# Blocks 3 and 4 of a state-space and Mish kernel: VectorE copies all partial sums of the projection, five rotations stand behind it, and GpSimd issues block 4's x after the stores of weight sums

## The chip, the cores and the metric

The kernel runs on one core of a Trainium2 chip. The metric is device time in microseconds (us) of one execution; the median of several executions counts. In the text PE is the matrix engine (TensorE), DVE is VectorE, ACT is ScalarE, POOL is GpSimd and SP is SyncE, which here issues DMA transfers only. Each of the five works through its own list of instructions strictly in the order in which the program gave them; they meet by semaphores.

## The reference

The input x has 2048 tokens of 1024 channels. With a layer norm over the channels, xn = (x - mean) / sqrt(var + eps), the result is the sum of three parts:

```
Bu   = xn @ B_bar^T                         # complex: two real projections, 1024 -> 1024 each
h[t] = Lam_bar * h[t-1] + Bu[t]             # a recurrence along the tokens, one complex state per channel
y    = 2 * real(h @ C^T) + xn * Dskip
m    = act @ w2,  act = hh * tanh(softplus(hh)),  hh = xn @ w1 + b1      # 1024 -> 3584 -> 1024
out  = x + y + m
```

## The kernel before, in words

**Blocks.** The 2048 tokens are worked in four blocks of 512; the code counts them as `blk` 0 to 3, the text calls them blocks 1 to 4. The change touches blocks 3 and 4 (`blk in SPLIT`, L183) and, for one group of transfers, block 2 (`blk == FAST`, which is 1).

**Stages of block 3 or 4 on PE.** (1) `first_tile` (L812): the first 12 of 28 tiles of xn @ w1, eight products of 512 columns each (L821). ACT writes tiles 0 to 6 with their bias into `hb` (L831), DVE tiles 7 to 11 (L834). (2) `project_fast` (L1124): the complex projection and the other 16 tiles of w1, both by a scheme that makes seven half-size products where eight would be plain (L901 for the projection, L972 for w1). (3) `dense` (L1214): act @ w2, 28 tiles f one after the other into all eight PSUM banks (L1211 with `act`). (4) `proj` (L1229): h @ C^T, eight channel groups j, into the same banks (L1211 with `hT`). (5) `finish` (L1274): DVE adds x, ACT issues the store.

**The order inside project_fast** is a string of tokens written out by hand (L185 to L188), and each engine's list follows it. `a` to `d` with a digit is one product of the projection, eight matmuls of 256 columns; each letter stands for two channel groups j. `w` to `z` with a digit is the same for four tiles of w1, with weights from `ring`. The digit says which of the seven products it is: 2, 1 and 5 open a bank, 6, 7, 4 go on in bank X behind product 1, and 3 goes on in bank Z behind 5. Before PE may go on in a bank, its partial sum must have been read out. That is done right behind the product, in `evacuate` (L905) or `w_evacuate` (L979): products 1, 5 and 6 are copied to a slot of `snaps`, products 1, 3 and 7 end with an addition on DVE (L926 or L1009), product 4 is copied out. For letters a and b the copies are DVE's (L916, L943), for c and d they are ACT's (L918, L945). For w to z most copies are ACT's (L992), a few DVE's (L995).

The other tokens: `r` n is `rotate_in` (L865), four DVE operations that turn channel group n by a table (L867 twice, L870, L872); `t1` is the tanh of the second chain (below); `g` n is a whole chain on ACT; `m` n multiplies a group of tiles on DVE (L859); `u` n lets PE do the first six tiles of `dense` for bank n.

```
HEAD = "a2 a1 b2 b1 a5 b5 a6 b6 a3 b3 a7 b7 c2 d2 a4 b4 c5 c1 r0 d5 d1 r1 c6 c3 d6"
PARTS = HEAD + (" t1 d3 c7 w1 d7 w5 w2 c4 d4 w6 r2 x1 x5 x2 w7 w3 r3 m0 x6 w4 y1 y5 y2 x7 x3 r4 m1 y6 x4"
                " z1 z5 g2 z2 y7 y3 z6 y4 u0 z7 u2 z3 u1 z4 u7 g3 r5 r6 r7")
```

**Chains** (`chain`, L844) make the activation on ACT for a group of tiles of `act`: Exp, Ln, Tanh, each over the whole group (L853). The groups are tiles 0 to 6, 7 to 11, 12 to 19 and 20 to 27. Chain 0 is called behind tile 6 of stage 1, chain 1 without its Tanh behind tile 11, chains 2 and 3 as g2 and g3.

**Behind project_fast** the main loop calls `recur(blk, j)` for j = 0 to 7 (L1173): two scans (L1176) and four operations that turn the state back (L1181, L1184, L1186), all on DVE. Behind recur 0 stands `chain_mul(2)`, behind recur 3 `chain_mul(3)` (L859): the products that `dense` reads as tiles f = 12 to 19 and f = 20 to 27.

**Block 2 prepares the weights** of the seven-product form. `w_load` brings raw parts of w1 into `hb` and `act`, `w_scale` (L1100) scales them on ACT, `w_sums` (L1108) makes sums and differences on DVE (L1120), and each result is stored to DRAM as `wsd` by a DMA that POOL issues (`w_store`, L1095, L1097). Parts for w1's third set lie in tiles 0 to 7 of `act`, so chain 0 of block 3 may write there only when those stores have landed. At the end of block 2 the calls come in this order: `w_scale(3)`, then `tail`'s rest, which ends with four loads of block 4's x issued by POOL (`load_x`, L360, called at L1311) into the tiles from which block 2's result is being stored, then `w_sums(2)` and `w_sums(3)` with four stores each, then block 3's `sums_x` (L1392): four subtractions on POOL into `TT` (L1395), which the projection reads.

Of the kernel before, what the change touches and what calls it, by code (L numbers as in the profile page):

```python
# [6 lines left out]
AF = mybir.ActivationFunctionType  # L7
# [156 lines left out]
def build_kernel(nc, A_x, A_Lambda_re, A_Lambda_im, A_B_re, A_B_im, A_C_re, A_C_im,  # L164
# [6 lines left out]
    NB = S // TB  # L171
    NQ = TB // P
# [8 lines left out]
    FAST = 1  # L181
# [2 lines left out]
    GROUPS = ((0, 7), (7, NPL), (NPL, NPL + 8), (NPL + 8, NF))  # L184
    HEAD = "a2 a1 b2 b1 a5 b5 a6 b6 a3 b3 a7 b7 c2 d2 a4 b4 c5 c1 r0 d5 d1 r1 c6 c3 d6"  # L185
    WHOLE = HEAD + " t3 d3 c7 d7 u7 c4 r2 u5 d4 u6 u4 r3 r4 r5 r6 r7 m2 m3"
    PARTS = HEAD + (" t1 d3 c7 w1 d7 w5 w2 c4 d4 w6 r2 x1 x5 x2 w7 w3 r3 m0 x6 w4 y1 y5 y2 x7 x3 r4 m1 y6 x4"
                    " z1 z5 g2 z2 y7 y3 z6 y4 u0 z7 u2 z3 u1 z4 u7 g3 r5 r6 r7")  # L188
    NWQ = (NF - NPL) // 4
    W_SEQ = [("wxyz".index(o[0]), int(o[1])) for o in PARTS.split() if o[0] in "wxyz"]  # L190
    W_BANKS = ((3, 5, 7), (1, 5, 6), (4, 5, 7), (3, 5, 6))
# [5 lines left out]
    PO = Queue(nc, "po")  # L197
# [162 lines left out]
    def load_x(queue, blk, q):  # L360
        r0 = blk * TB + q * P
        i = blk % 2
        queue.dma(lambda e: e.dma_start(xx[:, i, q, :], A_x[0, r0:r0 + P, :]),  # L363
                  s_xx[i][q] if blk else s_x0[q], writes=[b_xx[i][q]])
# [197 lines left out]
    def b1(f):  # L562
        return par[:, 3 * NJ + f:3 * NJ + f + 1]
# [43 lines left out]
    def w1_tile(base, f, k):  # L607

        s = (base + 2 * (f // 4) + k // (NK // 2)) % NRING
        wt = ring[:, s, :].rearrange("p (k f) -> p k f", k=NK // 2)  # L610
        return s, wt[:, k % (NK // 2), (f % 4) * P:(f % 4 + 1) * P]
# [185 lines left out]
    def mish_tanh(g):  # L797
        a = act[:, g * GF:(g + 1) * GF, :]
        aop(lambda e: e.activation(a, a, AF.Tanh), reads=[b_act[g]], writes=[b_act[g]])
# [8 lines left out]
    def item_done():  # L808
        n_item[0] += 1
        ring_load()  # L810

    def first_tile(blk, f):  # L812
        bank, hs = f % 8, f % (2 * GF)
        if blk in SPLIT:
            bank = (0, 1, 2, 3, 5, 1, 4, 0, 6, 2, 3, 7)[f]
        raw = blk == 0 and f < NR
        if raw:
            first_rest(f)
        for k in range(0 if raw else NK):
            s, w = w1_tile(n_item[0], f % 4, k)  # L820
            PE.mm(lambda e, k=k, w=w: e.matmul(ps[:, bank, :], lhsT=w, rhs=xnT[:, k, :],  # L821
                                               start=k == 0, stop=k == NK - 1),
                  reads=[b_ring[s]] + b_xnT, writes=[b_ps[bank]], first=k == 0, last=k == NK - 1)
        if f % 4 == 3:
            item_done()
            item_done()
        if f % GF == 0 and f >= 2 * GF:
            mish_mul(f // GF - 2)
        ts = slice(2 * P if raw else 0, 4 * P)
        if blk and f < GF:  # L830
            aop(lambda e: e.activation(hb[:, hs, :], ps[:, bank, :], AF.Identity, bias=b1(f)),  # L831
                reads=[b_ps[bank], b_par], writes=[b_hbf[hs]])
        else:
            vop(lambda e: e.tensor_scalar(hb[:, hs, ts], ps[:, bank, ts], b1(f), None, op0=ALU.add),  # L834
                reads=[b_ps[bank], b_par], writes=[b_hbf[hs]])
        if blk in SPLIT:
            if f == GF - 1:
                chain(0)
            if f == NPL - 1:
                chain(1, (0, 1))  # L840
        elif f % GF == GF - 1:
            mish(f // GF, hold=blk >= FAST and f == NF - 1)

    def chain(g, passes=(0, 1, 2)):  # L844
        lo, hi = GROUPS[g]
        i = lo - NPL if lo >= NPL else lo
        h, b_h = hb[:, i:i + hi - lo, :], b_hbf[i:i + hi - lo]
        a, b_a = act[:, lo:hi, :], b_actf[lo:hi]
        if lo >= NPL:
            h, b_h, a, b_a = a, b_a, h, b_h  # L850
        for n in passes:
            src, b_src, fn, bias = ((h, b_h, AF.Exp, 0.0), (a, b_a, AF.Ln, 1.0), (a, b_a, AF.Tanh, 0.0))[n]
            aop(lambda e, src=src, fn=fn, bias=bias: e.activation(a, src, fn, bias=bias), reads=b_src, writes=b_a)  # L853

    def chain_mul(g):
# [46 lines left out]
                    ps[:, bank, o:o + TH], lhsT=w, rhs=x, start=opens and begin, stop=end, skip_group_check=True),  # L902
                    reads=[b_w] + b_x, writes=[b_ps[bank]], first=begin, last=end, chained=not opens)

    def evacuate(pr, n, keep):  # L905
        X, Y, Z = (4 * ((pr + 1) % 2) + i for i in range(3))
        j0 = 2 * pr

        def bank(b):
            return ps[:, b, :].rearrange("p (j t) -> p j t", j=2)  # L910

        def snap(b):
            i = free_snaps.pop(0)
            dst = snaps[:, 2 * i:2 * i + 2, D - TH:D]
            if pr < 2:
                vop(lambda e: e.tensor_copy(dst, bank(b)), reads=[b_ps[b]], writes=[b_snap[i]])  # L916
            else:
                aop(lambda e: e.copy(dst, bank(b)), reads=[b_ps[b]], writes=[b_snap[i]])  # L918
            return dst, i

        def join(b, kept, ci, th):
            src, i = kept
            b_src = b_snap[i]
            free_snaps.append(i)
            dst = hT16[:, ci, j0:j0 + 2, th * TH:(th + 1) * TH]
            vop(lambda e: e.tensor_tensor(dst, bank(b), src, op=ALU.add),  # L926
                reads=[b_ps[b], b_src], writes=b_hT[ci][j0:j0 + 2])

        if n == 1:
            keep[pr, "a"] = snap(X)  # L930
            join(Y, keep[pr, "a"], 0, 0)
        if n == 5:
            keep[pr, "e"] = snap(Z)
        if n == 6:
            keep[pr, "v"] = snap(X)
        if n == 3:
            join(Z, keep[pr, "v"], 0, 1)
        if n == 7:
            join(X, keep[pr, "e"], 1, 1)
        if n == 4:  # L940
            dst = hT16[:, 1, j0:j0 + 2, 0:TH]
            if pr < 2:
                vop(lambda e: e.tensor_copy(dst, bank(X)), reads=[b_ps[X]], writes=b_hT[1][j0:j0 + 2])  # L943
            else:
                aop(lambda e: e.copy(dst, bank(X)), reads=[b_ps[X]], writes=b_hT[1][j0:j0 + 2])  # L945
# [162 lines left out]
    def w_sums(i):  # L1108
        (rl_, b_rl_), (rh_, b_rh_), (il_, b_il_), (ih_, b_ih_) = (w_unit(w_raw(i, ci, kh))
                                                                  for ci in range(2) for kh in range(2))  # L1110
        (s1, b_s1), (s2, b_s2), (s4, b_s4), (s3, b_s3) = (w_unit(u) for u in w_sum_at(i))
        for n, o, b_o, x, b_x, y, b_y, op in ((5, s1, b_s1, il_, b_il_, ih_, b_ih_, ALU.add),
                                              (6, s2, b_s2, s1, b_s1, rl_, b_rl_, ALU.subtract),
                                              (3, s4, b_s4, rh_, b_rh_, s2, b_s2, ALU.subtract),
                                              (7, s3, b_s3, rl_, b_rl_, il_, b_il_, ALU.subtract)):
            if n == 3:
                y = y.bitcast(f16)
            if n == 6:
                x = x.bitcast(f16)
            vop(lambda e, o=o, x=x, y=y, op=op: e.tensor_tensor(o.bitcast(f16), x, y, op=op),  # L1120
                reads=b_x + b_y, writes=b_o)
            w_store(i, n, o, b_o)

    def project_fast(order, open_unit):  # L1124
        keep = {}
        split = order is PARTS
        w_pos[0] = 0
        for o in order.split():
            kind, n = o[0], int(o[1:])
            if kind == "r":  # L1130
                rotate_in(n)
            elif kind == "u":
                open_unit(n)
            elif kind == "m":
                (chain_mul if split else mish_mul)(n)
            elif kind == "t":
                if split:
                    chain(n, (2,))
                else:
                    mish_tanh(n)  # L1140
            elif kind == "g":
                chain(n)
            elif kind in "wxyz":
                w_product("wxyz".index(kind), n)
                w_evacuate("wxyz".index(kind), n, keep)
            else:
                product("abcd".index(kind), n)
                evacuate("abcd".index(kind), n, keep)

    def project_in():  # L1150
        for j in range(NJ):
# [53 lines left out]
    def tail(blk, base):  # L1205
# [89 lines left out]
        if ends:  # L1295

            for h in range(2):
# [7 lines left out]
                r0 = blk * TB + 3 * P  # L1305
                out_events["end", h] = (SP, AC)[h].dma(lambda e, lo=lo, r0=r0: e.dma_start(
                    out[0, r0:r0 + P, lo:lo + 256], xx[:, i, 3, lo:lo + 256]), DmaSem(nc, "d_end%d" % h), reads=[b_end[h]])
        if blk >= FAST:
            for _ in range(njt):
                item_done()  # L1310
        if blk + 2 < NB:  # L1311
            for q in range(NQ):
                load_x(PO, blk + 2, q)

# [91 lines left out]
    for blk in range(NB):  # L1406
# [37 lines left out]
        if blk in SPLIT:  # L1444
            project_fast(PARTS, open_unit)
        elif blk:
# [75 lines left out]
        if blk == FAST:  # L1522
            w_sums(2)
            w_sums(3)
        if blk == FAST - 1:
            snaps_ready()

# [35 lines left out]
```

## Time and profile before

| | |
|---|---|
| median of 3 runs | 612.12 us (611.13 to 612.88) |
| the profiled execution | 611.5 us, its span 610.3 us |
| PE busy | 598.6 us, 98% |
| DVE busy | 489.5 us, 80% |
| ACT busy | 399.1 us, 65% |
| POOL busy | 124.3 us, 20% |
| the chain that ended last | PE 90%, DMA 3%, ACT 3%, DVE 2%, issue 2% |
| PE's waits over the whole span | for ACT's copies (L918) 5.0 us, once; for DVE 1.0 us and for DMA 0.9 us, both at the start |

A row of a timeline gives the start in us, the time in us, the engine, the line, the operation, the tiles that it writes and reads, how many were merged into the row, and in brackets how long the engine had been idle before it and what ended that. Within a merged row the operations follow on one another. Matmuls overlap: eight of 256 columns take 0.87 us from the start of the first to the start of what follows, though the row says 1.04.

### The profile page before, as it was taken

The page shows a single profiled execution, that of the slowest core. Times are in us where ns is not written, and L with a number is a line of the kernel's source. Part 1 is how long each engine was busy: PE and PEld are TensorE (multiplying, and loading weights), DVE is VectorE, ACT ScalarE, POOL GpSimd, SP SyncE. Part 2 cuts the span into 40 slices and gives each one's busy share as a digit, 9 for nine tenths or more (in the row PEclk, how much of TensorE's full clock was granted, in tenths as well). Part 3 has the DMA queues.
Part 4 walks back from the last instruction along what each step waited for, and adds up shares of the span by engine and source line. Part 5 has one row for each costly group of instructions (what it writes and reads, how often), then busy time and mean ns, then how long its engine had stood idle before and what let it go on. Part 6 is the DMA issues. An engine that isn't in the chain of part 4 may idle for free.

```text
span 610.3 us, 8878 instructions
## 1 busy us (share of the span) xinstructions
PE 598.6 (98%) x3393; PEld 334.9 (55%) x3439; DVE 489.5 (80%) x758; ACT 399.1 (65%) x376; POOL 124.3 (20%) x137
## 2 busy tenths in 40 slices
PE   8999999999999999999999889999999999999998
PEld 7644444444444586444445778644444688844444
DVE  6999999999998969969687468799707567789923
ACT  4589998389879898294572977995302968892000
POOL 2899300221025000610448000000004200000000
PEclk9999999999999999999999989999999999999999
DMA  8999996991795401899899118655666404854421
GB/s 247 253 279 272 244 172 183 293 294 60 216 330 179 170 21 31 261 303 275 230 389 407 53 36 273 212 172 169 173 192 199 163 1 144 286 192 142 166 73 69
DMA packets 103236, 119.36 MB, mean 196 GB/s; under 512 B 52890, under 2 KB 74010, under 8 KB 103194
## 3 DMA queue, kind: packets, MB, share of 16 engines
q1 hardware_dynamic: 93424, 91.05, 52.0%
q0 software_dynamic: 6080, 19.41, 9.5%
q10 hardware_dynamic: 3690, 8.34, 3.7%
q8 instruction: 27, 0.44, 0.3%
q14 instruction: 15, 0.12, 0.1%
HBM read 90.98 MB, written 15.73 MB: 175 GB/s over the span
## 4 chain that ended last, share of the span: by engine, by line
PE 90%; DMA 3%; ACT 3%; DVE 2%; issue 2%; SPq 1%; POOL 0%; ACTq 0%; DVEq 0%
PE ps L1211 49%; PE ps L821 17%; PE ps L901 9%; PE ps L972 8%; PE ps L1155 5%; ACT act L853 2%; DMA wsd<-act 2%; DMA ring<-in_B_w_dram 1%; PE ps L626 1%; DVE act L1120 1%; PE ps L617 0%; ACT L853 0%; DVE act L995 0%; POOL wsd L1097 0%; SPq L363 0%
## 5 line engine op out<-in xcount | busy, mean ns | idle before, releaser
L1211 PE MATMUL ps<-ring,act 128*128 128x512 bf16 x876 | 193.8, 379 | 1.1
L1211 PEld LDWEIGHTS ps<-ring,act 128*128 128x128 bf16 x896 | 87.7, 98 | 103.3
L821 PE MATMUL ps<-xnT,ring 128*128 128x512 bf16 x571 | 125.8, 379 | 0.7
L821 PEld LDWEIGHTS ps<-xnT,ring 128*128 128x128 bf16 x584 | 57.2, 98 | 68.7 <-DMA ring<-in_B_w_dram 0.2
L1211 PE MATMUL ps<-ring,hT 128*128 128x512 bf16 x369 | 81.6, 379 | 0.5
L1211 PEld LDWEIGHTS ps<-ring,hT 128*128 128x128 bf16 x378 | 37.0, 98 | 44.6
L1176 DVE TENSOR_TENSOR_SCAN hT<-cs,qi,hT 128x512 bf16<-128x512 f32 x48 | 58.9, 1267 | 0.0
L834 DVE TENSOR_SCALAR hb<-ps,par 128x512 bf16<-128x512 f32 (+1 forms) x59 | 39.3, 708 | 10.7 <-PE ps L821 10.2
L831 ACT ACTIVATE hb<-ps,par 128x512 bf16<-128x512 f32 x21 | 13.8, 689 | 45.2 <-PE ps L821 45.2
L1181 DVE TENSOR_TENSOR mt<-hT,tab 128x1024 bf16<-128x1024 bf16 x64 | 41.4, 688 | 1.1
L1395 POOL TENSOR_TENSOR TT<-xnT 128x1024 f16<-128x1024 bf16 x6 | 15.1, 2516 | 132.5 <-DVE mt L551 132.5
L1279 DVE TENSOR_TENSOR xx<-ps,xx 128x1024 bf16<-128x1024 f32 (+1 forms) x16 | 18.6, 1187 | 25.5 <-PE ps L1211 25.5
L926 DVE TENSOR_TENSOR hT<-ps,snaps 128x512 f16<-128x512 f32 x36 | 24.2, 688 | 14.2 <-ACT snaps L918 11.1
L972 PE MATMUL ps<-TT,ring 128*128 128x256 f16 x256 | 32.2, 273 | 0.0
L867 DVE TENSOR_TENSOR mt<-hT,tab 128x1024 bf16<-128x1024 f16 x48 | 30.9, 684 | 0.3
L792 ACT ACTIVATE act<-hb 128x3584 bf16<-128x3584 bf16 x8 | 25.5, 3184 | 6.8 <-DVE hb L834 6.8
L853 ACT ACT_TABLE_LOAD x18 | 23.1, 1283 | 10.3 <-DMA wsd<-act 10.0
L992 ACT ACTIVATE snaps<-ps,par,wsm 128x256 f32<-128x256 f32 x44 | 23.7, 560 | 8.9 <-PE ps L972 8.1
L901 PE MATMUL ps<-TT,SS 128*128 128x256 f16 x192 | 24.3, 279 | 5.0 <-ACT snaps L918 5.0
L853 ACT ACTIVATE hb<-hb 128x4096 bf16<-128x4096 bf16 x8 | 28.9, 3617 | 0.1
L1009 DVE SCALAR_TENSOR_TENSOR act<-ps,wsm,snaps 128x512 bf16<-128x512 f32 x24 | 17.8, 749 | 13.4 <-PE ps L972 9.8
L1155 PE MATMUL ps<-xnT,BT 128*128 128x512 bf16 x126 | 27.7, 379 | 0.1
(187 smaller groups left out, 973.2 us busy)
## 6 DMA issues: line engine op xcount, KB each, us to landing
ring<-in_B_w_dram SPq DMA_DIRECT2D x96, 512.0 KB, 4.5
ring<-wsd SPq DMA_DIRECT2D x28, 512.0 KB, 4.7
ring<-ctd SPq DMA_DIRECT2D x24, 512.0 KB, 3.5
wsd<-act POOLq DMA_DIRECT2D x20, 256.0 KB, 7.9
ctd<-act ACTq DMA_DIRECT2D x8, 512.0 KB, 4.3
out_dram<-xx ACTq DMA_DIRECT2D x15, 256.0 KB, 5.9
xx<-in_A_x_dram POOLq DMA_DIRECT2D x12, 256.0 KB, 6.2
act<-in_A_B_re_dram POOLq DMA_DIRECT2D x8, 256.0 KB, 5.1
```

What stands on the lines that cost most here:

```text
L792: aop(lambda e: e.activation(a, hs, AF.Exp), reads=[b_hb[g % 2]], writes=[b_act[g]])
L821: PE.mm(lambda e, k=k, w=w: e.matmul(ps[:, bank, :], lhsT=w, rhs=xnT[:, k, :], start=k == 0, stop=k == NK - 1), reads=[b_ring[s]] + b_xnT, ...
L834: vop(lambda e: e.tensor_scalar(hb[:, hs, ts], ps[:, bank, ts], b1(f), None, op0=ALU.add), reads=[b_ps[bank], b_par], writes=[b_hbf[hs]])
L853: aop(lambda e, src=src, fn=fn, bias=bias: e.activation(a, src, fn, bias=bias), reads=b_src, writes=b_a)
L867: vop(lambda e, s=s: e.tensor_tensor(mt[:, s, :, :], hT16[:, :, j, :], tab[:, s, j, :].unsqueeze(1).to_broadcast([P, 2, TB]), op=ALU.mult) ...
L901: PE.mm(lambda e, w=w, x=x, o=o, begin=begin, end=end: e.matmul(ps[:, bank, o:o + TH], lhsT=w, rhs=x, start=opens and begin, stop=end, ski ...
L926: vop(lambda e: e.tensor_tensor(dst, bank(b), src, op=ALU.add), reads=[b_ps[b], b_src], writes=b_hT[ci][j0:j0 + 2])
L972: PE.mm(lambda e, w=w, x=x, o=o, begin=begin, end=end: e.matmul(ps[:, bank, o:o + TH], lhsT=w, rhs=x, start=opens and begin, stop=end, ski ...
L1155: PE.mm(lambda e, j=j, ci=ci, k=k, bank=bank: e.matmul(ps[:, bank + ci, :], lhsT=BT[:, ci, j, k, :], rhs=xnT[:, k, :], start=k == 0, stop= ...
L1176: vop(lambda e, ci=ci, init=init: e.tensor_tensor_scan(out=hT[:, ci, j, :], data0=cj("r", j).to_broadcast([P, TB]), data1=hT[:, ci, j, :], ...
L1181: vop(lambda e, s=s: e.tensor_tensor(mt[:, s, :, :], hT[:, :, j, :], tab[:, s, j, :].unsqueeze(1).to_broadcast([P, 2, TB]), op=ALU.mult), ...
L1211: PE.mm(lambda e: e.matmul(ps[:, u, :], lhsT=lhsT, rhs=rhs, start=st_, stop=last), reads=reads, writes=[b_ps[u]], first=st_, last=last, te ...
```

## The change

The tokens t1 and r0 to r7 of PARTS move, for blocks 3 and 4 only. Before, r0 and r1 stood among the products of c and d, r2, r3 and r4 among those of w, x and y, and r5, r6, r7 at the end. After, r0, r1 and r2 stand in the three places among w, x and y, and r3 to r7 at the end. The Tanh of chain 1 follows its Exp and Ln at once. In these two blocks DVE makes the copies for c and d as well. Block 2 keeps its order and its engines (`split` is false there). POOL's four loads of block 4's x are issued after the eight stores of `w_sums(2)` and `w_sums(3)`.

```diff
-    PARTS = HEAD + (" t1 d3 c7 w1 d7 w5 w2 c4 d4 w6 r2 x1 x5 x2 w7 w3 r3 m0 x6 w4 y1 y5 y2 x7 x3 r4 m1 y6 x4"
-                    " z1 z5 g2 z2 y7 y3 z6 y4 u0 z7 u2 z3 u1 z4 u7 g3 r5 r6 r7")
+    PARTS = ("a2 a1 b2 b1 a5 b5 a6 b6 a3 b3 a7 b7 c2 d2 a4 b4 c5 c1 d5 d1 c6 c3 d6"
+             " d3 c7 w1 d7 w5 w2 c4 d4 w6 r0 x1 x5 x2 w7 w3 r1 m0 x6 w4 y1 y5 y2 x7 x3 r2 m1 y6 x4"
+             " z1 z5 g2 z2 y7 y3 z6 y4 u0 z7 u2 z3 u1 z4 u7 g3 r3 r4 r5 r6 r7")
...
             if f == NPL - 1:
-                chain(1, (0, 1))
+                chain(1)
...
-    def chain(g, passes=(0, 1, 2)):
+    def chain(g):
...
-        for n in passes:
-            src, b_src, fn, bias = ((h, b_h, AF.Exp, 0.0), (a, b_a, AF.Ln, 1.0), (a, b_a, AF.Tanh, 0.0))[n]
+        for src, b_src, fn, bias in ((h, b_h, AF.Exp, 0.0), (a, b_a, AF.Ln, 1.0), (a, b_a, AF.Tanh, 0.0)):
...
-    def evacuate(pr, n, keep):
+    def evacuate(pr, n, keep, on_v):
...
-            if pr < 2:
+            if on_v:
                 vop(lambda e: e.tensor_copy(dst, bank(b)), reads=[b_ps[b]], writes=[b_snap[i]])
             else:
                 aop(lambda e: e.copy(dst, bank(b)), reads=[b_ps[b]], writes=[b_snap[i]])
...
-            if pr < 2:
+            if on_v:
                 vop(lambda e: e.tensor_copy(dst, bank(X)), reads=[b_ps[X]], writes=b_hT[1][j0:j0 + 2])
...
             elif kind == "t":
-                if split:
-                    chain(n, (2,))
-                else:
-                    mish_tanh(n)
+                mish_tanh(n)
...
                 product("abcd".index(kind), n)
-                evacuate("abcd".index(kind), n, keep)
+                evacuate("abcd".index(kind), n, keep, split or kind in "ab")
...
-        if blk + 2 < NB:
+        if blk + 2 < NB and blk != FAST:
             for q in range(NQ):
                 load_x(PO, blk + 2, q)
...
         if blk == FAST:
             w_sums(2)
             w_sums(3)
+            for q in range(NQ):
+                load_x(PO, blk + 2, q)
```

## The prediction

> **What bounds the kernel now.** I read the page's busy times first, then PE's waits, then the timelines of PE, ACT and DVE around the one long wait. PE is busy for 598.6 of 610.3 us and waits once: 5.0 us for ACT's copies (L918), in block 3's projection. PE's timeline there, then block 4's at the same place:
>
> ```profile
> 331.03 3.66 PE L901 MATMUL ps<-xnT,BT 128*128 128x256 bf16 x32
> ...
> 347.62 1.04 PE L901 MATMUL ps<-xnT,BT 128*128 128x256 bf16 x8
> 353.67 1.89 PE L901 MATMUL ps<-TT,SS 128*128 128x256 f16 x8 [5.01 <-ACT snaps L918]
> 355.35 1.53 PE L901 MATMUL ps<-xnT,SS 128*128 128x256 bf16 x8
> ...
> 359.34 1.04 PE L972 MATMUL ps<-xnT,ring 128*128 128x256 bf16 x8
> ...
> 483.10 3.66 PE L901 MATMUL ps<-xnT,BT 128*128 128x256 bf16 x32
> ...
> 504.94 1.04 PE L972 MATMUL ps<-xnT,ring 128*128 128x256 bf16 x8
> ```
>
> From a2, the first product, to w1, the 26th, block 4 takes 504.94 - 483.10 = 21.84 us (0.873 per product) and block 3 takes 359.34 - 331.03 = 28.31. So the wait costs **6.47 us**, more than its length: c6, the 21st, was due at 331.03 + 20 x 0.873 = 348.49 and began at 353.67, 5.18 late; the other 1.29 come behind it, where c6 and c3 run slower. The clock says why: granted 1.00 in 348 to 352 us, 0.62 in 352 to 356, 0.96 in 356 to 360. ACT is late because its chain 0 began late:
>
> ```profile
> 333.29 1.28 ACT L853 ACT_TABLE_LOAD   x1 [10.01 <-DMA wsd<-act]
> ...
> 350.31 2.34 ACT L853 ACTIVATE act<-act 128x2560 bf16<-128x2560 bf16 x1
> 352.56 2.03 ACT L918 COPY snaps<-ps 128x512 f32<-128x512 f32 x4
> ...
> 358.39 1.28 ACT L853 ACT_TABLE_LOAD   x1
> 359.69 2.34 ACT L853 ACTIVATE act<-act 128x2560 bf16<-128x2560 bf16 x1
> ```
>
> The copies for c and d stand behind two chains (333.29 to 352.56), and these behind stores of weight sums (the chain that ended last: issue 321.75, landing 11.38 us later).
>
> **Edit 1: DVE makes the copies for c and d.** Per block eight operations leave ACT (0.58 each) and go to DVE (0.69 each, row L916), and r0 and r1 leave the same stretch. DVE then has 7 operations of about 0.66 per letter, 4 x 7 x 0.66 = 18.5 us against PE's 28 x 0.873 = 24.4. Followed one by one, with 0.19 us from a product's end to DVE's start (a1: 332.78 to 332.97): c1 ends at 346.74, its copy at 347.62, and c6, which goes on in that bank, is due at 348.49. The worst stretch (d5, d1, c6) leaves d6's and c7's banks free 0.6 and 1.1 us early. So PE's wait goes, and with it the slow clock. What is late next? ACT's first copy for w1, which w6 (32nd product, 358.1 without the wait) needs. With chain 0 at the old 333.29, ACT ends chain 1's Ln at 352.56, its Tanh, now at once, 3.54 us later (358.39 to 361.93 in the old place) at 356.10, and w1's copies at 357.2. That is 0.9 us early even if edit 3 brings nothing. In block 4 ACT is 8 us ahead and nothing waited: no gain. Term: **-6.47 us**. Bounds: 0 if another wait takes the place, -6.5 in full.
>
> **Edit 2: five rotations at the end instead of three.** DVE's list is in order, and at the end of project_fast it starts level with PE: the operation ahead of the rotations waits for the last product, z4. Before:
>
> ```profile
> 390.50 1.12 DVE L995 TENSOR_SCALAR act<-ps,wsm,par 128x256 bf16<-128x256 f32 x2 [1.42 <-PE ps L972]
> 391.54 1.28 DVE L867 TENSOR_TENSOR mt<-hT,tab 128x1024 bf16<-128x1024 f16 x2
> ...
> 393.65 1.29 DVE L867 TENSOR_TENSOR mt<-hT,tab 128x1024 bf16<-128x1024 f16 x2
> ...
> 395.77 1.29 DVE L867 TENSOR_TENSOR mt<-hT,tab 128x1024 bf16<-128x1024 f16 x2
> ...
> 402.26 2.28 DVE L859 TENSOR_TENSOR act<-act,hb 128x4096 bf16<-128x4096 bf16 x1
> ...
> 417.94 2.28 DVE L859 TENSOR_TENSOR act<-act,hb 128x4096 bf16<-128x4096 bf16 x1
> ```
>
> ```profile
> 390.29 44.62 PE L1211 MATMUL ps<-ring,act 128*128 128x512 bf16 x202
> 434.75 2.54 PE L1211 MATMUL ps<-ring,hT 128*128 128x512 bf16 x10
> ```
>
> DVE has no idle time from 390.50 to the second multiplication (L859), so the two added rotations, 2 x 2.115 = 4.23 us (391.54 to 393.65 to 395.77), move everything behind them by 4.23. Who waits? PE's dense stage reads tiles 12 to 19 after the first L859 and 20 to 27 after the second. It runs from 390.29 to 434.75, 206 matmuls in program order (6 for u7, 24 for the four other banks of tiles 0 to 5, then 8 per tile; four records are missing), 0.2158 us each. Tile 12 is matmul 78: 390.29 + 78 x 0.2158 = 407.12. The first L859 ends at 404.54: 2.58 us of room. Tile 20 is matmul 142: 420.93. The second ends at 420.22: **0.71 us of room**. With 4.23 more and 0.05 to release, PE waits 1.7 us at tile 12 (408.82 - 407.12); by tile 20 it is that much later and waits 1.9 more. Together 4.23 - 0.71 + 0.05 to 0.15 = 3.6 us. Block 4 has the same distances (dense from 535.89, L859 ending at 550.14 and 565.82): 3.6 again. Nothing later is hurt: the scans feed `proj`, which needs j = 0 at 434.75 and has it at 402.3, and j = 5 to 7 at 452, when recur 7 has ended at 438.5 (both now some 4 us later). Block 4's transposes of xn move from 435.4 to about 440, wanted at 462.5. Term: 2 x 3.6 = **+7.2 us**, bounds 6.0 to 8.0 (rooms misread by 0.3).
>
> **Edit 3: loads of x behind the stores.** POOL's list at the place:
>
> ```profile
> 313.67 0.54 POOL L1097 DMA_DIRECT2D wsd<-act  x1 [0.82 <-ACT act L1103]
> 314.20 0.54 POOL L363 DMA_DIRECT2D xx<-in_A_x_dram  x1
> ...
> 319.61 0.55 POOL L363 DMA_DIRECT2D xx<-in_A_x_dram  x1 [1.18 <-DVE mt L551]
> 320.14 4.27 POOL L1097 DMA_DIRECT2D wsd<-act  x8
> 324.43 2.14 POOL L1395 TENSOR_TENSOR TT<-xnT 128x1024 f16<-128x1024 bf16 x1
> ```
>
> The loads wait for block 2's output stores, and the eight wsd stores stand behind them although DVE has their data from 312.3 on (L1120). Moved ahead, the stores go at 314.2 to 318.5, the four loads at 318.5 to 320.6, and TT begins near 320.7 instead of 324.4 (it is first read by a5 at 334.5). The store that chain 0 waits for is issued near 315.8 instead of 321.75, and with 8 to 11 us to land chain 0 starts at 324 to 328 instead of 333.3. The x loads land before 330 and are read at 408. But by edit 1 the PE no longer cares when chain 0 starts, so: 0 us, bounds -0.1 and +0.9, the last if SP's ring loads land later in the fuller queue (DMA is near its full share from 304 to 336 us anyway, with POOL's queue never empty).
>
> **Sum.** 611.5 - 6.47 + 7.2 + 0 = 612.2 for the profiled execution. The median of the runs is 0.6 above that execution, so 612.8. The gain is real and given back later, by chance almost to the microsecond. With the terms' bounds and the spread of single runs (611.13 to 612.88) this case covers 611.0 to 614.5.
>
> **Rivals.** (a) *Clock*: the four new waits of 1.7 to 1.9 us close the clock gate as the 5.01 us did. Price up to 4 x 1.29 = 5.2: 618.0, slower. For it: a wait here did lower the clock. Against: the first ring wait of 0.69 us, near 6.9 us, left it at 1.00, and during the long wait it still stood at 1.00 in 348 to 352. The new waits are nearer to 0.69 than to 5.01; I take 0. The point is how much idle time the gate bears. The Trainium skill, "TensorE: Matmul & The Clock Gate", "What's actually happening", has half clock after an idle window of about 3.4 us, which the new waits don't fill; its section on a second failure mode, in which short idles make the clock swing, speaks against this change and would give the 618.0. (b) *The head still waits*, on DVE or on w1's copies: the 6.47 stay, 619.3 in full. Against: the rooms of 0.6 to 1.1 us above. (c) *The rotations cost PE nothing*, since multiplications come earlier than I place them: 612.1 - 6.5 = 605.6. For it: the page's idle PE time would allow it. Against: DVE starts level with z4 and nothing idles behind it. (d) *Edit 3 does not bring chain 0 forward*, the queue being as long as before: same time as the forecast.
>
> **Chances.** Forecast with (d) 0.72, (a) 0.09, (b) 0.08, (c) 0.11. About 0.3%, 1.8 us, can be told from no change. Within the forecast case, 0.60 is no change, 0.10 slower (above 613.9), 0.02 faster. Faster 0.02 + 0.11 = 0.13; slower 0.10 + 0.09 + 0.08 = 0.27; same 0.60. The range, 611.0 to 618.0, leaves out (c) and the full price of (b).
>
> **What would show it.** In the profile after: no wait of PE for L918 or any copy in block 3, a2 to w1 in 21.8 us; four waits of PE for DVE's multiplication (L859) in the dense stages, near 1.7, 1.9, 1.7, 1.9 us; DVE's five rotations back to back; the wait of ACT for wsd down from 10 us to under 5. Wrong would be: dense stages without waits (c), a clock under 1.00 behind the short waits (a), or a new releaser in block 3's head (b).

## The result and the profile after

The changed kernel takes 615.32 us (median of 17 runs, 612.03 to 620.77) against 612.57 of the kernel before (17 runs, 609.26 to 617.77). The ratio is **1.0054, 95% interval 1.0028 to 1.0081**: about 3.3 us slower (1.7 to 5.0). The forecast was 612.8 with "no change" likeliest; the time lies within the stated range of 611.0 to 618.0, but above the 611.0 to 614.5 of the forecast case, and the difference is beyond the 1.8 us that were to count as no change. The profiled execution took 614.75 us, its span is 613.5.

PE's waits of the changed kernel (engine, line, who released it, us in total, times, longest):

```profile
PE ps L1208 <- DVE act L859: 6.6, 4, 1.7
PE ps L822 <- DMA ring<-in_B_w_dram: 2.3, 1, 2.3
PE ps L580 <- DVE filler L412: 1.0, 1, 1.0
...
```

The last row shown and those left out are waits in the first 12 us. The wait for ACT's copies is gone, and four waits for DVE's multiplication have come, as forecast. The second row was not forecast: in block 3's first tiles PE waits for a ring load of w1. The timeline of PE, the three places after one another:

```profile
327.44 6.22 PE L822 MATMUL ps<-xnT,ring 128*128 128x512 bf16 x28 [2.27 <-DMA ring<-in_B_w_dram]
333.50 3.66 PE L901 MATMUL ps<-xnT,BT 128*128 128x256 bf16 x32
...
350.96 1.04 PE L901 MATMUL ps<-TT,SS 128*128 128x256 f16 x8
...
355.33 1.04 PE L972 MATMUL ps<-xnT,ring 128*128 128x256 bf16 x8
...
404.87 13.99 PE L1208 MATMUL ps<-ring,act 128*128 128x512 bf16 x64 [1.58 <-DVE act L859]
420.55 13.99 PE L1208 MATMUL ps<-ring,act 128*128 128x512 bf16 x64 [1.70 <-DVE act L859]
434.38 27.79 PE L1208 MATMUL ps<-ring,hT 128*128 128x512 bf16 x128
```

Read it against the timeline shown before. From a2 to w1 PE now takes 355.33 - 333.50 = 21.83 us, where it took 28.31: 6.48 gained. From w1 to the first matmul on `hT` it takes 434.38 - 355.33 = 79.05, where it took 434.75 - 359.34 = 75.41: 3.64 lost; in block 4 the dense stage loses 3.61 (48.08 us against 44.47). A wait in the brackets is counted from the modelled end of the last matmul, 0.16 us behind its place in the stream, so 1.58 + 1.70 + 2 x 0.16 = 3.60. And a2 starts at 333.50 where it started at 331.03, though tile 0 starts alike (310.33 and 310.31): 2.45 lost to the ring load. The sum is -6.48 + 3.64 + 3.61 + 2.45 = +3.22, and the spans of the two profiled executions differ by 3.2. Nothing is left over.

DVE at the end of block 3's project_fast, the rows that stand for those shown of before:

```profile
386.49 1.12 DVE L995 TENSOR_SCALAR act<-ps,wsm,par 128x256 bf16<-128x256 f32 x2 [1.42 <-PE ps L972]
387.54 1.28 DVE L867 TENSOR_TENSOR mt<-hT,tab 128x1024 bf16<-128x1024 f16 x2
...
389.65 1.29 DVE L867 TENSOR_TENSOR mt<-hT,tab 128x1024 bf16<-128x1024 f16 x2
...
396.02 1.29 DVE L867 TENSOR_TENSOR mt<-hT,tab 128x1024 bf16<-128x1024 f16 x2
...
402.52 2.28 DVE L859 TENSOR_TENSOR act<-act,hb 128x4096 bf16<-128x4096 bf16 x1
...
418.21 2.28 DVE L859 TENSOR_TENSOR act<-act,hb 128x4096 bf16<-128x4096 bf16 x1
```

It still starts level with z4 (a wait of 1.42 for PE), then five rotations follow back to back from 387.54. From 387.54 to the first L859 it is 14.98 us, before 402.26 - 391.54 = 10.72. ACT of the changed kernel:

```profile
322.62 0.69 ACT L832 ACTIVATE hb<-ps,par 128x512 bf16<-128x512 f32 x1 [1.04 <-PE ps L822]
323.59 1.28 ACT L853 ACT_TABLE_LOAD   x1 [0.28 <-DMA wsd<-act]
...
344.26 2.34 ACT L853 ACTIVATE act<-act 128x2560 bf16<-128x2560 bf16 x1
356.41 1.16 ACT L992 ACTIVATE snaps<-ps,par,wsm 128x256 f32<-128x256 f32 x2 [9.81 <-PE ps L972]
```

Chain 0 starts 9.7 us earlier: ACT writes the last of its input (tile 6) until 323.31 and then waits only 0.28 us for the store, where it waited 10.01. Once both chains are done, ACT stands idle for 9.8 us. That is the gain of the third edit, at a place where no one waits.

### The profile page after: what moved, and what is told of

It is laid out like the page before. It is cut to its first block, busy times and chain, and to the rows that moved or that the text cites. A ratio compares the mean times of both kernels' runs of the same rounds, so it can differ in the third digit from the quotient of the medians.

```text
span 613.5 us, 8910 instructions
## 1 busy us (share of the span) xinstructions
PE 600.6 (98%) x3439; PEld 334.2 (54%) x3439; DVE 503.7 (82%) x774; ACT 391.0 (64%) x360; POOL 123.8 (20%) x137
## 4 chain that ended last, share of the span: by engine, by line
PE 84%; DVE 11%; DMA 4%; SPq 1%; issue 0%
PE ps L1208 39%; PE ps L822 18%; PE ps L901 12%; PE ps L972 8%; PE ps L1152 5%; DMA ring<-in_B_w_dram 4%; DVE hT L1173 3%; DVE mt L867 2%; DVE mt L1178 2%; DVE act L859 1%; PE ps L627 1%; DVE hT L870 1%; DVE hT L872 1%; DVE hT L1181 1%; PE ps L618 0%; DVE hT L1183 0%
## 5 line engine op out<-in xcount | busy, mean ns | idle before, releaser
L1208 PE MATMUL ps<-ring,act 128*128 128x512 bf16 x896 | 196.0, 379 | 6.6 <-DVE act L859 6.6
L832 ACT ACTIVATE hb<-ps,par 128x512 bf16<-128x512 f32 x21 | 13.8, 691 | 45.8 <-PE ps L822 45.8
L1208 PE MATMUL ps<-CT,hT 128*128 128x512 bf16 x128 | 27.8, 379 | 0.0
L972 PEld LDWEIGHTS ps<-TT,ring 128*128 128x128 f16 (+1 forms) x256 | 25.0, 98 | 3.8
```

The costliest lines, as they stand in the source:

```text
L972: PE.mm(lambda e, w=w, x=x, o=o, begin=begin, end=end: e.matmul(ps[:, bank, o:o + TH], lhsT=w, rhs=x, start=opens and begin, stop=end, ski ...
L1208: PE.mm(lambda e: e.matmul(ps[:, u, :], lhsT=lhsT, rhs=rhs, start=st_, stop=last), reads=reads, writes=[b_ps[u]], first=st_, last=last, te ...
```

## The experiments

The theory after the result: three terms, copies on DVE -6.5, rotations at the end +7.2, loads behind the stores +2.4. The rivals: the late ring load is jitter; or DVE's lateness comes from the copies and not from the rotations. Eight kernels take the terms apart. All ratios are to the kernel before on the same chip.

**loads_back**: the changed kernel, third edit undone.

```diff
-        if blk + 2 < NB and blk != FAST:
+        if blk + 2 < NB:
...
             w_sums(3)
-            for q in range(NQ):
-                load_x(PO, blk + 2, q)
```

> The changed kernel with one part undone: the loads of block 4's x are issued ahead of the stores of w_sums(2) and w_sums(3) again. Theory (sum of three terms: copies on DVE -6.5, two more rotations at the end +7.2, loads behind the stores +2.4 by a late ring load of w1 in block 3's first tiles): the DMA wait of PE near tile 8 of block 3 goes (0.3 us or less), the four waits for L859 stay at 6.6 us in the view of waits, chain 0 of block 3 begins near 333 us again without PE waiting for it; about 0.7 us above the kernel before, 2.4 below the changed kernel. Rival (the late ring load is jitter of single executions and has nothing to do with the order of POOL's list): as the changed kernel, 2.5 to 3 us above the kernel before, with the DMA wait there again.

Measured: 612.14 us, ratio 1.0007 (0.9989 to 1.0026). PE's waits:

```profile
PE ps L1208 <- DVE act L859: 6.5, 4, 1.7
PE ps L580 <- DVE filler L412: 1.0, 1, 1.0
```

The wait for the ring load is gone and the waits for DVE are there in full. Chain 0 starts at 332.94, late as in the kernel before, and PE doesn't wait for it: that part of the forecast holds. Without the third edit the change is the tie that the forecast had computed.

**loads_only**: the kernel before with the third edit alone (three lines).

> The kernel before with one part done alone: the loads of block 4's x behind the stores of w_sums(2) and w_sums(3). Theory: chain 0 of block 3 begins near 324 us, ACT has ended chain 1's Ln near 343 and makes the copies for c and d in time, so PE's wait of 5.0 us for L918 and the slow clock behind it go without any copy on DVE (-6.5); the rotations stay three at the end, so no wait for L859; the late ring load costs up to 2.4: 4.1 us below the kernel before. Rival 1 (the late ring load is jitter): 6.5 below as a rule. Rival 2 (PE's wait for L918 has another cause than the late chain 0): as the kernel before or 2.4 above it.

Measured: 606.72 us, ratio 0.9916 (0.9896 to 0.9935), 5.1 us faster (0.0084 x 612). PE's waits:

```profile
PE ps L821 <- DMA ring<-in_B_w_dram: 4.3, 2, 2.8
PE ps L579 <- DVE filler L411: 1.0, 1, 1.0
...
```

So the late chain 0 is what made ACT late for the copies of c and d: with the stores first it starts at 327.94 (later than the 324 expected, still early enough), and L918 costs PE nothing though ACT still makes the copies; a2 to w1 takes 357.79 - 335.95 = 21.84 us. The price of the edit is the longer of the two waits in the first row, 2.8 us at 329.90; the other, 1.5 us, lies at 53 us in block 1, far ahead of the edit. This one edit does better than the whole change.

**rot_hidden**: the changed kernel with two rotations moved into gaps of DVE's list.

```diff
-             " d3 c7 w1 d7 w5 w2 c4 d4 w6 r0 x1 x5 x2 w7 w3 r1 m0 x6 w4 y1 y5 y2 x7 x3 r2 m1 y6 x4"
-             " z1 z5 g2 z2 y7 y3 z6 y4 u0 z7 u2 z3 u1 z4 u7 g3 r3 r4 r5 r6 r7")
+             " d3 c7 r0 w1 d7 w5 w2 c4 d4 w6 r1 x1 x5 x2 w7 w3 r2 m0 x6 w4 y1 y5 y2 x7 x3 r3 m1 y6 x4"
+             " z1 z5 g2 z2 y7 y3 z6 y4 u0 z7 r4 u2 z3 u1 z4 u7 g3 r5 r6 r7")
```

> The changed kernel with two of its rotations moved into gaps of DVE's list: r0 behind c7, r1 to r3 in the three old places, r4 behind z7, so that three stand at the end as in the kernel before. Theory: the four waits for L859 (7.2 us with the matmul's own end) go, the DMA wait of block 3's first tiles stays: 7.2 below the changed kernel, 4 below the kernel before. Rival (it is the eight copies per block, not the place of the rotations, that make DVE late): the waits for L859 stay, time as the changed kernel.

Measured: 606.78 us, ratio 0.9922 (0.9897 to 0.9947). PE's waits:

```profile
PE ps L822 <- DMA ring<-in_B_w_dram: 2.6, 1, 2.6
PE ps L618 <- DMA ring<-in_B_w_dram: 1.2, 1, 1.2
PE ps L580 <- DVE filler L412: 1.0, 1, 1.0
PE ps L822 <- DVE hb L835: 0.4, 1, 0.4
```

No wait for L859 is left, with all copies still on DVE; so the rotations' place made DVE late, and the copies did not. The wait for the ring load stays, 2.6 us in the profiled execution.

**rot_hidden_loads_back**: both edits together.

> Both edits of the two runs named rot_hidden and loads_back: copies for c and d on DVE, three rotations at the end, loads of block 4's x ahead of the stores. Theory: only the gain is left, 6.5 us below the kernel before, PE without any wait over 0.3 us after the start. Rival (the late chain 0 of block 3 now delays ACT's first copies for w1, since its Tanh stands ahead of them): a wait of PE at w6 in block 3 of 1 us or more.

Measured: 605.95 us, ratio 0.9897 (0.9878 to 0.9916): 6.3 us faster than the kernel before, the term of the copies alone. PE's waits:

```profile
PE ps L618 <- DMA ring<-in_B_w_dram: 1.4, 1, 1.4
PE ps L580 <- DVE filler L412: 1.0, 1, 1.0
PE ps L822 <- DMA ring<-in_B_w_dram: 0.7, 1, 0.7
```

The 0.7 us, against the 0.3 expected as the most, is a wait at 53 us in block 1; in block 3's first tiles PE doesn't wait for the ring load, and nowhere for a copy. The difference from rot_hidden is 0.25%, but the two intervals overlap.

**rot_only**: the kernel before with r0 to r7 in the changed kernel's places, copies on ACT.

> The kernel before with the rotations alone moved as in the changed kernel (five at the end); the copies for c and d stay on ACT, Tanh of chain 1 behind d6, loads ahead of the stores. Theory: four waits of PE for L859, 1.6 to 1.7 us each by the view of waits, 7.2 us in all, beside the old wait of 5.0 us for L918: 7.2 above the kernel before (619.6). Rival (DVE is late at the end only because it also makes the copies): no waits for L859, time as the kernel before.

Measured: 620.17 us, ratio 1.0131 (1.0111 to 1.0151), 8.0 us slower; 7.2 lies within the interval.

```profile
PE ps L1212 <- DVE act L860: 6.5, 4, 1.7
PE ps L902 <- ACT snaps L919: 5.4, 1, 5.4
...
```

The same four waits without any copy of c or d on DVE, beside the old one.

**copies_only**: the kernel before with the copies on DVE, rotations where they were.

```diff
-            if pr < 2:
+            if on_v:
...
-                evacuate("abcd".index(kind), n, keep)
+                evacuate("abcd".index(kind), n, keep, split or kind in "ab")
```

> The kernel before with the copies for c and d alone moved to DVE in blocks 3 and 4; all rotations stay where they were, r0 behind c1 and r1 behind d1. Theory (DVE's list followed by hand: r0 and r1 push the copies of d1 to 351.7 and of c6 to 355.1, where d6 and c7 want them at 350.2 and 352): PE waits for DVE's copies some 3.3 us in each of the two blocks, so block 3 gains 6.5 and loses 3.3 and block 4 loses 3.3: within 1 us of the kernel before. Rival (the copies can go to DVE with the rotations in their old places, since 18.5 + 4.2 us of DVE fit into PE's 24.4): 6.5 below the kernel before.

Measured: 611.84 us, ratio 0.9993 (0.9977 to 1.0010). The timeline of PE in block 3, d6 and c7:

```profile
352.51 1.05 PE L901 MATMUL ps<-TT,SS 128*128 128x256 f16 x8 [1.21 <-DVE snaps L916]
...
355.83 1.05 PE L901 MATMUL ps<-TT,BT 128*128 128x256 f16 x8 [1.40 <-DVE snaps L916]
```

The waits fall on the two products that following the list by hand had named, 1.4 and 1.6 us with the 0.16, 2.9 of the 3.3 expected, and the same again in block 4. So r0 and r1 had to leave the stretch where DVE makes the copies; a sum of busy times (18.5 + 4.2 us within 24.4) would have called it free.

**loads_far**: as rot_hidden, the loads of x behind block 3's subtractions.

```diff
                     if blk >= FAST:
                         sums_x(at.index(f))
+                    if blk == FAST + 1 and f == at[-1]:
+                        for q in range(NQ):
+                            load_x(PO, blk + 1, q)
```

> As rot_hidden (stores of w_sums first), but the loads of block 4's x are issued only behind block 3's four subtractions, some 10 us later still, so that they are no part of the crowd before 330 us. Theory (the stores, issued earlier, take the DMA engines' turns from the ring load of w1): the second of the two ring loads that are issued near 310 lands 17 to 18 us after its issue as in rot_hidden, PE waits for it 2 us or more, time within 1 us of rot_hidden. Rival (the loads of x, now in one burst, crowd it out): it lands 14 to 15 us after its issue, the wait goes, time as rot_hidden_loads_back.

Measured: 606.68 us, ratio 0.9917 (0.9898 to 0.9935), as rot_hidden. The ring load lands 16.3 us after its issue, less than the 17 expected, and PE waits 0.9 us, less than the 2 expected. It is not back at 14 to 15 though the loads of x, issued from 333 us, can't be in its way. So the stores are, in size less than the theory had it; whether the other 1.8 us of rot_hidden's 18.1 come from the loads of x or from the spread of single executions, this one profile can't tell.

**loads_mid**: as rot_hidden, the loads of x between the stores of w_sums(2) and those of w_sums(3).

> As rot_hidden, but the loads of block 4's x stand between the stores of w_sums(2) and those of w_sums(3). Theory: half of the moved stores come early, so the ring load lands between the two cases (15 to 17 us after its issue) and PE waits up to 1.5 us, 0.5 to 1 below rot_hidden; chain 0 of block 3 starts near 324 to 327. Rival (any store of w_sums ahead of the loads does the whole harm): as rot_hidden.

Measured: 606.07 us, ratio 0.9911 (0.9883 to 0.9938). The ring load lands 13.8 us after its issue and PE doesn't wait for it: here the theory's "between" missed, since four early stores did no harm in the profiled execution. Chain 0 starts at 326.66. In time the kernel can't be told from rot_hidden and its neighbours.

**The ring load, over all kernels.** The second of two loads issued near 310 us lands so many us after its issue in the profiled executions:

| loads of x ahead of the stores | us | stores first | us |
|---|---|---|---|
| before | 15.1 | changed kernel | 17.7 |
| loads_back | 14.4 | loads_only | 18.2 |
| rot_only | 14.2 | rot_hidden | 18.1 |
| copies_only | 14.4 | loads_far | 16.3 |
| rot_hidden_loads_back | 13.7 | (loads_mid, half the stores first) | 13.8 |

Each number is of one execution, but the five and the four don't overlap, so the lateness follows the order of POOL's list and is hardly jitter. In time the price shows between loads_back and the changed kernel, whose intervals don't overlap; rot_hidden and rot_hidden_loads_back can't be told apart. What moved meanwhile: the DMA queues from the issue of that load to its landing (packets, MB, share of 16 engines), first in the changed kernel (309.7 to 327.4 us), then in loads_back (309.15 to 323.6):

```profile
q0 software_dynamic: 1248, 4.10, 60.2%
q1 hardware_dynamic: 1294, 1.94, 29.0%
```

```profile
q0 software_dynamic: 799, 2.62, 48.8%
q1 hardware_dynamic: 1268, 1.85, 34.0%
```

The ring loads are in q1, which moves nearly the same, 1.9 MB, in both. POOL's queue q0 moves 1.5 MB more ahead of the landing when the stores come first; at the 395 GB/s of the window that is 3.7 us, and the landing is 3.3 us later. That is more than the longer window would bring: q0 moves 232 GB/s instead of 181, q1 110 instead of 128. In the first fence the two queues move nearly as many packets, 1248 and 1294, and q1 with its smaller packets gets less than half the bytes of q0. With the loads of x ahead, q0 falls behind. In loads_back, from 315.5 to 317.5 us:

```profile
q1 hardware_dynamic: 484, 0.49, 68.7%
q0 software_dynamic: 57, 0.19, 25.7%
```

In that kernel POOL stands idle ahead of three of the four loads, for 1.13, 2.12 (from 315.4 to 317.6) and 3.59 us, the last time until an output store of block 2 has landed. That these pauses are why q0 moves so few packets fits, but no run takes them alone. The Trainium skill, "DMA: Bandwidth & Descriptors", "Queues, rings and completion order", says that an engine takes turns between its queues packet by packet; the nearly equal counts of the first fence agree. The bytes of q0 are not the whole account either: after its issue rot_hidden's ring load lands 4.3 us later than that of rot_hidden_loads_back (18.06 and 13.74), and up to the landing q0 moves 0.9 MB more (3.45 and 2.56) and q1 0.8 MB more (2.37 and 1.60). How the rest of the lateness arises stays open.

## Why the prediction was right and wrong

- **The wait for ACT's copies costs 6.47 us and goes.** Right: 6.48 in the trace, 6.3 in time by rot_hidden_loads_back. The rooms held: no PE wait for a copy in loads_back, where chain 0 is as late as before.
- **Two more rotations move both multiplications by 4.23 us, PE waits 1.7 + 1.9 us per block.** Right: 1.74 and 1.86 with the 0.16, in both blocks; 3.64 and 3.61 of the 3.6 forecast.
- **The loads behind the stores: 0 us, bounds -0.1 and +0.9.** This is the step that failed. The text saw that ring loads might land later, and set that aside because DMA was near its full share anyway and POOL's queue never empty. But a full share of all queues together says nothing about how they divide it: in loads_back q0 has transfers in flight throughout and still moves 1.5 MB less up to the landing than in the changed kernel. The price was 2.45 us in the profiled execution, and the bound should have come from the landing's own room: in the kernel before, the ring load landed at 324.78 for a matmul due at 310.31 + 68 x 0.2158 = 324.99 (tile 8's second half), 0.2 us of room. The rest of that step held: the store that chain 0 waits for landed early, and no one gained from it in this kernel. Block 4's x landed from 330 to 334 us instead of before 330, which cost nothing.
- **The sum** then was +0.7 for the median and is +2.8 (612.57 to 615.32), +3.3 by the ratio; the failed term makes up the difference. That the time still fell within the stated range is luck: the range was stretched to 618.0 for rival (a), and the late ring load was priced at 0.9 at most.
- **Rivals.** (a) The clock behind the four short waits stays at 1.00 (400 to 408, 416 to 424, 552 to 560 and 568 to 576 us): it was right to cost them at nothing. (b) and (c) did not occur. Nor did (d): chain 0 came forward by 9.7 us.
- **What the prediction did not ask** is which edit would do alone. loads_only shows that the first wait could be had by the third edit, without moving any copy.

## What to carry to other kernels

When an in-order engine starts a stretch level with PE, every operation that is added there appears downstream in full, less the smallest room of the readers behind it. Here the rooms were 2.58 us at tile 12 and 0.71 at tile 20, so of the two rotations' 4.23 us about 3.6 were lost, in each of two blocks. A group of DMAs that is moved forward can be paid for by transfers that share the DMA engines with it: look up which landing has the least room, and not only whether the DMA is busy. And when several edits aim at one wait, measure each alone: here one made the other two needless for that wait.

## What the runs showed of the hardware that was not expected

A wait shorter than the 5.01 us of the kernel before can lower PE's clock too, but doesn't always. The wait of 2.65 us in rot_hidden did. Its PE row and the stages around it (the last three numbers of a stage are the granted clock, the DMA share and GB/s):

```profile
328.29 7.90 PE L822 MATMUL ps<-xnT,ring 128*128 128x512 bf16 x28 [2.65 <-DMA ring<-in_B_w_dram]
```

```profile
core 0: us, PE busy (x) PEld busy (x) DVE busy (x) ACT busy (x) POOL busy (x), PEclk, DMA share, GB/s
326.00:328.00 2.00, 0.00 (x0) 0.00 (x0) 2.00 (x1) 0.05 (x1) 2.00 (x2) 1.00 1.01 397
328.00:330.00 2.00, 1.71 (x5) 0.70 (x6) 1.90 (x2) 1.99 (x2) 2.00 (x2) 0.61 1.02 393
330.00:332.00 2.00, 2.00 (x7) 0.66 (x5) 1.23 (x2) 2.00 (x1) 2.00 (x2) 0.53 1.03 420
332.00:334.00 2.00, 2.00 (x11) 0.91 (x10) 0.75 (x1) 1.97 (x3) 0.55 (x1) 1.00 1.02 416
```

The clock falls to about half behind the wait, and 28 matmuls take 7.90 us where the changed kernel's take 6.22: the wait costs 1.7 us more than its length. The waits of 2.27 us in the changed kernel's profiled execution and of 2.82 in loads_only left the clock at 1.00. Over the 17 runs of the changed kernel nine have a mean granted clock of 1.00 (median 614.1 us) and eight of 0.994 to 0.997 (median 618.0), while in loads_back 11 of 12 have 1.00. Over all kernels with the stores first (the changed kernel, loads_only, rot_hidden, loads_far) 13 of 41 runs have less than 1.00; with the loads of x first and no wait for L918 (loads_back, rot_hidden_loads_back, copies_only) it is 1 of 27. That the longer runs are those in which the wait for the ring load lowered the clock fits, and rot_hidden's profiled execution (0.997) is one of them, but only profiled executions show the wait itself, so for the others it is not shown. The Trainium skill, "TensorE: Matmul & The Clock Gate", "What's actually happening", has the clock fall after an idle window of about 3.4 us; the 2.65 us of rot_hidden are shorter, so here the measurement differs from the page.
